# Input rows and modulation weights issued by ScalarE, modulation products in 32-column pieces

## The chip, the cores and the metric

The kernel runs on one core of one Trainium2 chip. The metric is the device time of one execution in microseconds (us), and of several runs the median. All arithmetic that matters here is fp32.

## The reference

The block is an adaLN layer around an S4D convolution and a token-mixing MLP, for L = 2048 tokens, D = 448 channels, N = 256 states, F = 1792 hidden units:

```python
mod = (_silu(c) @ w_mod).reshape(1, 6, 1, -1)        # c: 1 x 448, w_mod: 448 x 2688
sa, ca, ga, sb, cb, gb = mod[:, 0], ..., mod[:, 5]
h = _layernorm(x) * (1 + ca) + sa
x = x + ga * S4D(h)     # y = irfft(rfft(h) * rfft(K)) + h * D_skip, K = 2 Re sum_n C exp(A dt l)
h = _layernorm(x) * (1 + cb) + sb
x = x + gb * MLP(h)     # over the token axis: w2 gelu(w1 h + b1) + b2
```

The change concerns the six modulation vectors `mod[k]` (k = 0 to 5, each of 448 numbers, needed on all 128 partitions) and the way in which the input `x` and the matrix `w_mod` come into the chip's memory.

## The kernel before

The first part of the program makes the convolution kernel K in 56 half groups, one in each step `s` of a long loop, and lays the rest of the first part (layer norm, transforms, modulation) between them. Every eighth step begins with a `window(s)`, in which ScalarE (ACT) makes the eight magnitudes of the next steps (`mag`, L614). A step then has these pieces:

- PE: `st_kgen(s - 2)` (L678, 32 small products into 32-column tiles), then `st_phase(s + 1)` (L603), which fills two pairs of accumulators, `xe` and `xg`, for the next step. There are two of each, so the phase of step s + 1 needs those of step s - 1 to be free: `xg` is free when VectorE (DVE) has done its last product of that step (L657).
- ACT: six activations (L644 to L649) on `xe` and `xg`; the first is `ab`, the third writes what DVE reads first.
- GpSimd (POOL): two products `G` (L651, L652), and `w` and `m` of a later step (L630, L632).
- DVE: two products `E` (L653, L654), then whatever `between` gives it, then two more (L656, L657). For s = 2 to 7 `between` holds the statistics of rows 2s and 2s + 1 of the input (`u_stats`, L494), so these must have landed; and pieces of the next chain of exponents (L384 to L397).

In window 8 the input is normalised and from then on `u_rows` makes products `pu` of the input (L525), which DVE multiplies by a modulation (`yt`, L528). Such a product, the accumulators of the modulations (`pm`) and those of `y` share one pool of three.

PE, ACT, DVE and POOL run their instructions in the order in which the code is written. SyncE (SP), which issues most transfers, does so too until step 8; after that a scheduler orders it.

Transfers issued by SP or ACT take one of eight completion semaphores, `DMAHW0` to `DMAHW7`, in turn, one turn for both engines together. Where a transfer takes a semaphore that an earlier transfer has used, the issuing engine first waits until that earlier one has landed. Transfers issued by POOL have eight semaphores of their own.

The 16 rows that each partition holds of the input (`xt`) come in by `x_load(r0, n, eng)`, which issues four transfers of 32 partitions each. Rows 0 to 3 are issued by POOL early; rows 4 to 7 after step 0 and rows 8 to 15 after step 1, by POOL as well. The four blocks of `w_mod` for k = 0 to 3 come in by `wm_load`: k = 1 by SP before step 0, k = 2, 3 and 0 by POOL before steps 2, 3 and 5 (the table `late`). The blocks for k = 4 and 5 are loaded later into `xt` by SP.

`modulation(k)` is four accumulated products of 112 x 448 by `scb`, the silu of c copied along 128 columns, so that every partition gets the sum; ACT then copies the accumulator to `mod[k]`. k = 1, 2 and 3 are made in halves in steps 2 to 7, k = 0 in window 8, k = 4 and 5 at the head of window 16.

Of the kernel before, what the change touches and what calls it, by code (L numbers as in the profile page):

```python
# [11 lines left out]
F32 = mybir.dt.float32  # L12
# [9 lines left out]
L, D, N, F = 2048, 448, 256, 1792  # L22
P = 128
# [193 lines left out]
def tile_adaln_s4d_mixer(ctx, tc, i, out):  # L217
# [20 lines left out]
    with ExitStack() as es:  # L238
# [76 lines left out]
        def wm_load(k, tile, eng=nc.sync):  # L315
            wms[k] = tile
            eng.dma_start(wms[k], i["w_mod"][:, k * D : (k + 1) * D].rearrange("(q p) d -> p q d", p=PP))
# [11 lines left out]
        def wm_slot(k):  # L329
            w = wm0.rearrange("p k d -> p (k d)")[0:PP]  # L330
            return w[:, 4 * D * (k % 4) : 4 * D * (k % 4 + 1)].rearrange("p (q d) -> p q d", q=4)
# [1 line left out]


        late = {
            2: lambda: wm_load(2, wm_slot(2), G),
            3: lambda: wm_load(3, wm_slot(3), G),
            5: lambda: wm_load(0, wm_slot(0), G),
            6: lambda: [
                nc.sync.dma_start(wu, i["WU"]),  # L340
                nc.sync.dma_start(wc, i["WC"].rearrange("p (c m) -> p c m", c=2)),
# [127 lines left out]


        sc = qp.tile([PP, 4], F32, name="sc")
        scb = qp.tile([PP, 4, P], F32, name="scb")

        pmods = {}

        def modulation(k, *halves):
            if 0 in halves:
                pmods[k] = pms.tile([P, D], F32, tag="ms", name="pm")
            for h in halves:
                for q in (2 * h, 2 * h + 1):  # L480
                    T.matmul(pmods[k], scb[:, q], wms[k][:, q], start=q == 0, stop=q == 3)
            if 1 not in halves:
                return
            pm = pmods.pop(k)
            act.append(lambda: S.activation(mod[k], pm, AF.Copy, bias=1.0 if k in (1, 4) else 0.0))


# [320 lines left out]
        def remainder():  # L808

            ts(dt4[:, 1:4], dt[:, 1:4], 1.0 / (4 * math.pi), None, ALU.mult)  # L810
            ts(ldt2[:, 1:4], ldt[:, 1:4], 1.5 * math.log(2.0), None, ALU.add)

            ts(sc, sc, 1.0, None, ALU.add)
            V.reciprocal(sc, sc)
            tt(sc, sc, cvec, ALU.mult)
            V.tensor_copy(scb, sc[:, :, None].to_broadcast([PP, 4, P]))

# [97 lines left out]
        par_load(1)  # L917
        for g in (1, 2):
            load(g, False)
        wm_load(1, wm_slot(1))  # L920
        remainder()

        def chains():
# [46 lines left out]
        def window(s):  # L970
            angle()
            logs(s == 8)
            if s == 8:
                u_scale()
                u_norm(0)
                u_norm(1)

            if s in (8, 16):
                for k in (0,) if s == 8 else (4, 5):
                    modulation(k, 0, 1)  # L980
            if s == 0:
                st_exponents(s)
            for e in range(BATCH):
                st_exp(s + e)

                if e + 1 < BATCH:
                    st_exponents(s + e + 1)
                else:
                    st_phase(s)
                mellow()  # L990
                if s == 8 and e == 0:
                    tt(mod[1], mod[1], mod[2], ALU.mult)
                flush(dve)
                flush(act)
                if s < 32:
                    more(WPACE[s // 8][e])
                if s == 0 and e >= 4:
                    u_stats(e - 4)
                if s == 8 and e == 1:

                    tt(mod[0], mod[0], mod[2], ALU.mult)
                if s and e < (2 if s <= 32 else 1):
                    st_kgen(s - (2 if s <= 32 else 1) + e)
                elif e == 5:
                    if s == 8:
                        yks[0] = y0.tile([P, 32, DC], F32, tag="yk", name="yk0")
                    st_s1(s > 16)

                if s in (8, 16):
                    some(u_rows, rows, (2, 2, 2, 2, 2, 0, 1, 1)[e])  # L1010
                elif s == 24 and e != 5:
                    some(u_cols, cols, 1)

                if s >= 40 and e == 2:
                    piece(False)
                if s >= 32 and e in (4, 7):
                    piece(e == 4 and pieces[0] < NP, V)
                if s == 0 and e in (4, 5):
                    st_mag2(e - 4)
                elif s and (e < 2 or s >= 32):  # L1020
                    st_mag2(s + e)
                if s == 8 and e == 0:
                    u_norm(e + 2)
                if s == 0 and e == 3:
                    for r in range(4):
                        dsk_copy(r)
            if s == 0:

                S.activation(one, one, AF.Sin)
# [6 lines left out]
        for s in range(tail):  # L1036
# [23 lines left out]
            def between():  # L1060
# [4 lines left out]
                if s < len(pace):  # L1065
                    more(pace[s])

            mellow()
            if s >= NHALF:
                flush(dve)  # L1070
# [15 lines left out]


            if s < 2:
                x_load(4 + 4 * s, 4 + 4 * s, G)
            free = s > 7 and not st_s1(s % BATCH == BATCH - 1)  # L1090
            if s + 2 < 32 and (s + 2) % BATCH > 1:
                st_mag2(s + 2)

            if 1 < s < 8:
                modulation(s // 2, s % 2)
            if s == 7:
                par_load(2)

# [265 lines left out]
```

## Time and profile before

| | before |
|---|---|
| median of 3 runs | 715.01 us (712.2 to 716.16) |
| the profiled execution | 720.78 us, of it span 719.0 us |
| busy PE, DVE, ACT, POOL | 632.4, 453.2, 438.7, 273.6 us |
| mean granted TensorE clock | 0.921 |

The profile is of one execution. In a row of the timeline stand the start (us from the start of the span), the duration, the engine, the line of the code, the operation, what it writes and reads, and in brackets how long the engine had been idle and what ended that. Rows of SP and POOL with DMA are the issue of a transfer, not the transfer itself. PEclk in a table by windows is the granted TensorE clock, 1.00 for full speed.

### The profile page before, as it was taken

To read this page: it belongs to the slowest core of one execution; us is meant where nothing else is said; L and a number is where in the kernel's file an instruction comes from. 1 tells how busy PE (TensorE), PEld (TensorE's weight loads), DVE (VectorE), ACT (ScalarE), POOL (GpSimd) and SP (SyncE) were. 2 spreads that over 40 slices of the span, in tenths; PEclk is the share of its full clock that TensorE was granted. 3 is DMA by queue.
4 is the path that set the end of the run, shared out by engine and by line. 5 is a ranking of instruction groups with operands and counts; after the bars stand their busy time and mean duration, and the time that the engine had idled before them with its cause. 6 is when DMAs were issued, how large, how long until landed. Compare 5 with 4: busy or idle time off the path is not lost. (4 is left out here: it accounts for less than half of the span.)

```text
span 719.0 us, 18288 instructions
## 1 busy us (share of the span) xinstructions
PE 632.4 (88%) x7204; PEld 456.4 (63%) x7204; DVE 453.2 (63%) x875; ACT 438.7 (61%) x876; POOL 273.6 (38%) x328
## 2 busy tenths in 40 slices
PE   0659889979989888799888949999999999999997
PEld 0335335434535556566565617778999999999996
DVE  7469879679778668586684548778622263334441
ACT  5847588887987789989883549787522242222220
POOL 6486437528737787878785600000000000000000
PEclk9868857988998889999899959999999999999999
DMA  7795464266888635535236989974585436655540
GB/s 169 207 191 131 162 192 138 113 229 179 244 227 248 204 92 133 149 100 154 70 102 181 285 245 266 239 195 113 174 231 146 148 109 172 173 155 154 156 139 26
DMA packets 101635, 121.19 MB, mean 169 GB/s; under 512 B 13066, under 2 KB 87422, under 8 KB 101422
## 3 DMA queue, kind: packets, MB, share of 16 engines
q1 hardware_dynamic: 100014, 113.16, 55.2%
q0 software_dynamic: 1536, 6.87, 4.4%
q8 instruction: 57, 0.93, 0.6%
q14 instruction: 28, 0.23, 0.1%
HBM read 84.64 MB, written 34.87 MB: 166 GB/s over the span
## 5 line engine op out<-in xcount | busy, mean ns | idle before, releaser
L202 ACT CAST whi<-w 128x896 fp32r<-128x896 f32 x64 | 59.7, 938 | 131.4 <-PE o L1331 84.7
L651 POOL TENSOR_TENSOR G<-mag,gs 128x512 f32<-128x512 f32 x56 | 71.9, 1284 | 92.4 <-ACT gs L647 92.1
L211 DVE TENSOR_TENSOR wlo<-w,whi 128x896 fp32r<-128x896 f32 x64 | 68.0, 1087 | 40.3 <-ACT whi L202 31.0
L603 PE MATMUL xg<-tab,lph 64*128 64x512 f32 x112 | 68.8, 617 | 25.9 <-ACT xg L649 8.0
L1196 PE MATMUL acc<-h3h,whi 128*128 128x448 f32 x224 | 83.3, 372 | 0.1
L1197 PE MATMUL acc<-h3l,whi 128*128 128x448 f32 x224 | 81.9, 366 | 0.0
L1331 PE MATMUL o<-ul,whi 128*128 128x448 f32 x224 | 81.3, 363 | 0.0
L1330 PE MATMUL o<-uh,whi 128*128 128x448 f32 x224 | 81.2, 362 | 0.0
L1198 PE MATMUL acc<-h3h,wlo 128*128 128x448 f32 x224 | 80.9, 361 | 0.0
L1332 PE MATMUL o<-uh,wlo 128*128 128x448 f32 x224 | 80.6, 360 | 0.0
L678 PEld LDWEIGHTS kg<-E,G 128*32 128x32 f32 x3584 | 59.8, 119 | 32.3 <-issue 16.4
L603 PE MATMUL xe<-tab,lph 64*128 64x512 f32 x112 | 67.8, 609 | 12.2 <-ACT gs L648 10.2
L678 PE MATMUL kg<-E,G 128*32 128x64 f32 x3584 | 69.8, 235 | 2.2 <-issue 1.5
L652 POOL TENSOR_TENSOR G<-mag,gs 128x512 f32<-128x512 f32 x56 | 71.7, 1280 | 0.0
L653 DVE TENSOR_TENSOR E<-m,xe 128x512 f32<-128x512 f32 x56 | 38.3, 683 | 40.8 <-ACT xe L646 31.8
L632 POOL TENSOR_TENSOR m<-mag,w 128x512 f32<-128x512 f32 x56 | 59.9, 1070 | 6.0 <-DVE E L657 1.5
L1334 DVE SCALAR_TENSOR_TENSOR y<-o,b,mod 128x448 f32<-128x448 f32 x16 | 10.9, 684 | 80.3 <-PE o L1332 80.3
L644 ACT ACTIVATE ab<-xe 128x512 f32<-128x512 f32 x56 | 33.7, 601 | 30.3 <-PE xe L603 16.1
L1196 PEld LDWEIGHTS acc<-h3h,whi 128*128 128x128 f32 x224 | 42.3, 189 | 13.8 <-ACT h L1252 6.3
L603 PE MATMUL xe<-tab,lex 64*128 64x512 f32 x56 | 31.7, 575 | 18.8 <-POOL dsk L468 17.2
L614 ACT ACTIVATE mag<-xe 128x512 f32<-128x512 f32 x56 | 35.5, 634 | 19.7 <-PE xg L603 14.0
L603 PEld LDWEIGHTS xg<-tab,lph 64*128 64x128 f32 x112 | 24.3, 217 | 36.3 <-issue 10.3
(229 smaller groups left out, 1486.1 us busy)
## 6 DMA issues: line engine op xcount, KB each, us to landing
w<-in_B_w_dram SPq DMA_DIRECT2D x64, 224.0 KB
w<-in_B_w_dram SPq DMA_DIRECT2D x32, 448.0 KB
yu_d<-yt SPq DMA_DIRECT2D x16, 448.0 KB
yi<-yu_d SPq DMA_DIRECT2D x32, 224.0 KB
us_d<-uo SPq DMA_DIRECT2D x16, 448.0 KB
u<-us_d SPq DMA_DIRECT2D x32, 224.0 KB
v_d<-vt SPq DMA_DIRECT2D x32, 224.0 KB
vt<-v_d SPq DMA_DIRECT2D x16, 448.0 KB
```

What stands on the lines that cost most here:

```text
L211: eng.tensor_tensor(lo, w, hi.bitcast(F32), ALU.subtract)
L603: T.matmul(out[k], lhs[r], rhs[r], start=start, stop=stop)
L632: G.tensor_tensor(m2, me, w[:, :, None].to_broadcast([P, GD, 32]), ALU.mult)
L651: G.tensor_tensor(Gt[:, 1], mg_, v32(sg), ALU.mult)
L652: G.tensor_tensor(Gt[:, 0], mg_, v32(cg_), ALU.mult)
L678: T.matmul(kgs[g][32 * q : 32 * q + 32, m], Gt[:, c, d], E[:, c, d], start=h == 0 and c == 0 and m == 0, stop=h == 1 and c == 1, skip_grou ...
L1196: nc.tensor.matmul(acc[f], hi[:, fs], h3h[:, r], start=r == 0, stop=False)
L1197: nc.tensor.matmul(acc[f], hi[:, fs], h3l[:, r], start=False, stop=False)
L1198: nc.tensor.matmul(acc[f], lo[:, fs], h3h[:, r], start=False, stop=r == 15)
L1330: nc.tensor.matmul(o, hi[:, ks], uh[kh][:, k], start=kh == 0 and k == 0, stop=False)
L1331: nc.tensor.matmul(o, hi[:, ks], ul[kh][:, k], start=False, stop=False)
L1332: nc.tensor.matmul(o, lo[:, ks], uh[kh][:, k], start=False, stop=kh == 1 and k == 6)
```

## The change

The rows 4 to 15 come in three parts of four, all issued by ACT: the first part before the activations of step 0, the second after step 0, the third after step 1. The modulation weights for k = 0 to 3 are issued by ACT too: k = 1 and 2 after the third part, k = 0 before step 3, k = 3 before step 4. `modulation` becomes two functions. `mod_parts(k)` makes the four products side by side, each with 32 columns of `scb` and into 32 partitions of one accumulator, and ACT copies that accumulator to `mod[k]`. `mod_sum(k)` multiplies the copy by a matrix `add4` that has ones in rows 0, 32, 64 and 96 and so adds the four pieces on every partition; ACT writes `mod[k]` anew from that. DVE writes `add4` at the start of the program.

```diff
         late = {
-            2: lambda: wm_load(2, wm_slot(2), G),
-            3: lambda: wm_load(3, wm_slot(3), G),
-            5: lambda: wm_load(0, wm_slot(0), G),
+            2: lambda: wm_load(2, wm_slot(2), S),
+            3: lambda: wm_load(0, wm_slot(0), S),
+            4: lambda: wm_load(3, wm_slot(3), S),
...
-        scb = qp.tile([PP, 4, P], F32, name="scb")
-
-        pmods = {}
-
-        def modulation(k, *halves):
-            if 0 in halves:
-                pmods[k] = pms.tile([P, D], F32, tag="ms", name="pm")
-            for h in halves:
-                for q in (2 * h, 2 * h + 1):
-                    T.matmul(pmods[k], scb[:, q], wms[k][:, q], start=q == 0, stop=q == 3)
-            if 1 not in halves:
-                return
-            pm = pmods.pop(k)
+        scb = qp.tile([PP, 4, 32], F32, name="scb")
+        add4 = qp.tile([P, P], F32, name="add4")
+        V.memset(add4, 0.0)
+        for q in range(4):
+            V.memset(add4[32 * q : 32 * q + 1], 1.0)
+
+        def mod_parts(k):
+            pm = pms.tile([P, D], F32, tag="ms", name="pm")
+            for q in range(4):
+                T.matmul(pm[32 * q : 32 * q + 32], scb[:, q], wms[k][:, q], start=True, stop=True)
+            act.append(lambda: S.copy(mod[k], pm))
+
+        def mod_sum(k):
+            pm = pms.tile([P, D], F32, tag="ms", name="pm")
+            T.matmul(pm, add4, mod[k], start=True, stop=True)
             act.append(lambda: S.activation(mod[k], pm, AF.Copy, bias=1.0 if k in (1, 4) else 0.0))
...
-            V.tensor_copy(scb, sc[:, :, None].to_broadcast([PP, 4, P]))
+            V.tensor_copy(scb, sc[:, :, None].to_broadcast([PP, 4, 32]))
...
-        wm_load(1, wm_slot(1))
         remainder()
...
-            if s in (8, 16):
-                for k in (0,) if s == 8 else (4, 5):
-                    modulation(k, 0, 1)
+            if s == 16:
+                mod_parts(4)
+                mod_parts(5)
...
                     tt(mod[0], mod[0], mod[2], ALU.mult)
+                    mod_parts(3)
+                elif s == 8 and e == 2:
+                    mod_sum(3)
+                elif s == 16 and e == 0:
+                    mod_sum(4)
+                    mod_sum(5)
...
+            if s == 0:
+                x_load(4, 4, S)
             mellow()
...
             if s < 2:
-                x_load(4 + 4 * s, 4 + 4 * s, G)
+                x_load(8 + 4 * s, 4, S)
+            if s == 1:
+                wm_load(1, wm_slot(1), S)
...
-            if 1 < s < 8:
-                modulation(s // 2, s % 2)
+            if 4 < s < 8:
+                mod_sum((1, 2, 0)[s - 5])
+            if 4 <= s < 7:
+                mod_parts((1, 2, 0)[s - 4])
```

What this does to the order of an engine is seen at three places. On ACT at the start of step 0 (`one` ends window 0, `ab` begins the step; what an instruction waits for stands in brackets) there stood before:

```order
33 L1029 ACT_TABLE_LOAD
34 L1029 ACTIVATE one<-one 128x1
35 L644 ACTIVATE ab<-xe 128x512 [waits PE_49]
36 L645 ACTIVATE gs<-xg 128x512 [waits PE_49]
37 L646 ACTIVATE xe<-xe 128x512 [waits Activation_49]
```

And now:

```order
33 L1037 ACT_TABLE_LOAD
34 L1037 ACTIVATE one<-one 128x1
35 L292 DMA xt<-in_A_u_dram 32x1792 [waits DMAHW3_49]
36 L292 DMA xt<-in_A_u_dram 32x1792 [waits DMAHW7_49]
37 L292 DMA xt<-in_A_u_dram 32x1792 [waits DMAHW5_49]
38 L292 DMA xt<-in_A_u_dram 32x1792 [waits DMAHW3_49]
39 L647 ACTIVATE ab<-xe 128x512 [waits PE_49]
```

Four issues stand ahead of the step, the first and the fourth on the same semaphore. After step 1 six more stand ahead of `ab` of step 2 (of after, with the last two of the four of `xt` and both of `wm`):

```order
59 L292 DMA xt<-in_A_u_dram 32x1792 [waits DMAHW4_49]
60 L292 DMA xt<-in_A_u_dram 32x1792 [waits DMAHW3_49]
61 L317 DMA wm_79<-in_w_mod_dram 112x4x448 [waits DMAHW6_49]
62 L317 DMA wm_79<-in_w_mod_dram 112x4x448 [waits DMAHW7_49]
63 L647 ACTIVATE ab<-xe 128x512 [waits PE_49,Activation_49]
```

Their semaphores were last used by transfers of SP. On SP, from the loads of the second group's parameters on to the reloads for later steps (`lph` feeds the phases of two steps each, `lex` those of window 8), before:

```order
42 L271 DMA A_A_imag<-in_A_A_imag_dram 128x256 [waits DMAHW1_49]
43 L589 DMA lph_143<-pars_57 32x256 [waits DMAHW3_49,DMAHW2_49]
44 L593 DMA lph_143<-pars_57 64x1x256 [waits DMAHW5_49,DMAHW4_49]
45 L589 DMA lph_144<-pars_57 32x256
46 L593 DMA lph_144<-pars_57 64x1x256
47 L317 DMA wm_79<-in_w_mod_dram 112x4x448 [waits DMAHW6_49]
48 L589 DMA lph_142<-pars_57 32x256 [waits DMAHW7_49,PE_49]
```

And after, with the reloads that follow:

```order
42 L271 DMA A_A_imag<-in_A_A_imag_dram 128x256 [waits DMAHW3_49]
43 L592 DMA lph_143<-pars_57 32x256 [waits DMAHW4_49]
44 L596 DMA lph_143<-pars_57 64x1x256 [waits DMAHW6_49,DMAHW5_49]
45 L592 DMA lph_144<-pars_57 32x256 [waits DMAHW7_49]
46 L596 DMA lph_144<-pars_57 64x1x256 [waits DMAHW0_49]
47 L592 DMA lph_142<-pars_57 32x256 [waits DMAHW1_49,PE_49]
48 L596 DMA lph_142<-pars_57 64x1x256 [waits DMAHW2_49,PE_49]
49 L592 DMA lph_143<-pars_57 32x256 [waits DMAHW4_49,DMAHW2_49,PE_49]
50 L596 DMA lph_143<-pars_57 64x1x256 [waits DMAHW6_49,DMAHW3_49,PE_49]
51 L592 DMA lex_145<-pars_57 32x256 [waits DMAHW5_49]
52 L596 DMA lex_145<-pars_57 64x1x256 [waits DMAHW6_49]
53 L592 DMA lex_146<-pars_57 32x256 [waits DMAHW7_49]
```

The load of `wm` is gone from SP, and the semaphores have shifted: `A_A_imag` (row 42) now takes `DMAHW3` after ACT's first transfer of `xt`, and ACT's fourth takes it after `A_A_imag`. By the same count ACT's twelfth transfer of `xt` (`DMAHW3`, row 60) follows SP's row 50, which waits for the phase of step 3, and the two of `wm` follow SP's rows 52 and 53.

On PE at the head of window 16 (`y` ends the step before, `xe` and `xg` belong to the window, `kg` is st_kgen, `pu` feeds DVE) there stood before:

```order
356 L481 MATMUL pm<-xt,scb 128x448 x8
357 L603 MATMUL xe<-tab,lex_145 128x512
358 L603 MATMUL xg<-tab,lex_145 128x512
359 L678 MATMUL kg<-E,G 32x64 x32
360 L525 MATMUL pu<-xt,wu 64x448 x4
```

And now:

```order
358 L482 MATMUL pm<-xt,scb 32x448 x8
359 L606 MATMUL xe<-tab,lex_145 128x512
360 L606 MATMUL xg<-tab,lex_145 128x512
361 L487 MATMUL pm<-mod_69,add_175 128x448
362 L487 MATMUL pm<-mod_70,add_175 128x448
363 L681 MATMUL kg<-E,G 32x64 x32
364 L528 MATMUL pu<-xt,wu 64x448 x4
```

Eight products of 128 columns become eight of 32 columns, and two summing products come after the window's first phase, behind ACT's copies of the pieces. In steps 4 to 8 the same replacement is made one modulation at a time: parts in steps 4, 5, 6 (k = 1, 2, 0), sums in steps 5, 6, 7, and k = 3 in window 8.

## The prediction

> **What bounds the kernel now.** First the page's busy times, then the windows (us, busy of each engine with instructions, PEclk, DMA share, GB/s) around the steps that the change touches.
>
> ```profile
> PE 632.4 (88%) x7204; PEld 456.4 (63%) x7204; DVE 453.2 (63%) x875; ACT 438.7 (61%) x876; POOL 273.6 (38%) x328
> 40.00:51.00 11.00, 3.58 (x72) 1.80 (x69) 5.40 (x9) 3.48 (x7) 9.81 (x13) 0.77 1.00 209
> 51.00:60.00 9.00, 8.55 (x83) 4.47 (x83) 8.86 (x19) 3.63 (x7) 5.48 (x6) 0.52 0.75 136
> 60.00:71.00 11.00, 10.96 (x226) 6.02 (x222) 9.41 (x20) 9.83 (x20) 7.00 (x7) 1.00 0.49 132
> ```
>
> PE's 88% is an average. From 40 to 51 us PE, DVE and ACT all stand half idle or worse while the transfers are at 1.00; then PE is full, first at half clock. The queues' share of the transfers' time between 40 and 46 us says whose they are, and the timelines of POOL, DVE and PE what they hold up.
>
> ```profile
> q0 software_dynamic: 142, 1.32, 98.0%
> 32.64 2.01 POOL L292 DMA_DIRECT2D xt<-in_A_u_dram  x4
> 45.85 0.63 DVE L494 BATCH_NORM_STATS2 st<-xt 128x6 f32<-128x448 f32 x1 [5.53 <-DMA xt<-in_A_u_dram]
> 47.34 2.58 DVE L392 TENSOR_TENSOR ya<-ya,xa 128x256 f32<-128x256 f32 x1
> 50.67 0.67 DVE L657 TENSOR_TENSOR E<-m,xg 128x512 f32<-128x512 f32 x1
> 51.45 0.76 PE L603 MATMUL xg<-tab,lph 64*128 64x512 f32 x1 [7.87 <-issue]
> 53.45 3.35 PE L481 MATMUL pm<-wm,scb 112*128 112x448 f32 x4
> ```
>
> POOL issues rows 4 to 7 at 32.64 us, and they land 11 to 13 us later. DVE waits 5.53 us for them in step 2; with a slow product (2.58 us) behind that, step 2's last product ends at 51.34 us, and only then does `xg` come free for PE's phase of step 4. That stall would go with rows that land earlier. PE then pays 3.35 us for two modulation products at half clock.
>
> **The transfers.** The changed kernel takes them from POOL; ACT issues sixteen. The nearest prices are SP's: 0.59 us for the same 224 KB of `xt` later in the program, and for a block of `wm` the 0.43 us of an ordinary load (the third row).
>
> ```profile
> L1138 SPq DMA_DIRECT2D xt<-in_A_u_dram x16: 528/590/613, 409.1 to 471.0; - x16
> 1.20 0.42 SPq L271 DMA_DIRECT2D A_C_real<-in_A_C_real_dram  x1
> 1.66 0.43 SPq L271 DMA_DIRECT2D A_C_imag<-in_A_C_imag_dram  x1
> 3.31 0.42 ACT L851 ACTIVATE xa<-A_C_real 128x256 f32<-128x256 f32 x1 [1.29 <-DMA A_C_real<-in_A_C_real_dram]
> 5.04 0.42 ACT L852 ACTIVATE ya<-A_C_imag 128x256 f32<-128x256 f32 x1 [1.31 <-DMA A_C_imag<-in_A_C_imag_dram]
> SPq L593 <- DMA lex<-pars: 1.9, 1, 1.9
> ```
>
> Issue alone is 12 x 0.59 + 4 x 0.43 = 8.8 us of ACT. But the order shows a dearer thing: the shared completion semaphores make an issuing engine wait for another's transfer. The last row is such a wait in the kernel before: SP's load of `lph` stood 1.9 us until a load of `lex`, with which it has no data in common, had landed. Now ACT is in that turn, with its activations behind it. How long a landing takes on this queue: from 1.20 to 3.31 is 2.1 us for 128 KB, from 1.66 to 5.04 is 3.4 us beside others. I take 2.6 for the first two waits, where 224 KB parts run beside them, and 2.1 for the small load later; both ends stay for the range.
>
> ```profile
> 28.05 0.58 ACT L644 ACTIVATE ab<-xe 128x512 f32<-128x512 f32 x1
> 31.65 0.60 ACT L644 ACTIVATE ab<-xe 128x512 f32<-128x512 f32 x1
> 26.69 0.43 SPq L271 DMA_DIRECT2D A_A_imag<-in_A_A_imag_dram  x1
> 38.45 0.68 DVE L657 TENSOR_TENSOR E<-m,xg 128x512 f32<-128x512 f32 x1
> 40.63 0.49 SPq L593 DMA_DIRECT2D lph<-pars  x1
> 42.18 0.54 SPq L589 DMA_DIRECT2D lex<-pars  x1
> ```
>
> *Step 0.* ACT issues its first part at 28.05. SP, which came to `A_A_imag` at 26.69, must wait until that has landed: 30.65. `A_A_imag` lands 2.6 later, at 33.25, and only then goes ACT's fourth: `ab` begins at 33.84 instead of 28.05. Without the two waits it would be 28.05 + 4 x 0.59 = 30.41.
>
> *Step 1.* A step and what stands behind it took 3.60 us (28.05 to 31.65); four issues add 2.36. `ab` of step 1: 39.80 (31.65 before). Its sixth activation ends 3.1 later, two products of DVE take 1.3: its last product ends at 44.2. PE's phase of step 3 follows, and SP's reload of `lph` behind that phase started 1.5 us after that product (39.13 to 40.63): here at 45.7.
>
> *Step 2.* ACT is free at 42.9 and has issued three parts by 44.7. The twelfth waits for that reload; the two of `wm` wait for the `lex` loads behind it. SP issued the last of these 1.55 us after the reload (40.63 to 42.18), so here at 45.7 + 1.55 = 47.25; it lands 2.1 later, and with one issue of 0.43 `ab` of step 2 stands at 49.8. DVE now needs three activations (1.5), two products (1.2), then what took 5.49 from 45.85 to 51.34. The statistics find their rows landed, at no cost, and the slow product (2.58 us beside POOL's work) I price at 1.2 like L384 in the row below: 5.49 - 2.58 + 1.2 = 4.1. Step 2 ends at 56.6 against 51.34: 5.3 later.
>
> ```profile
> 31.79 1.18 DVE L384 TENSOR_TENSOR s<-xa,ya 128x256 f32<-128x256 f32 x1 [0.80 <-ACT ya L383]
> 54.85 0.68 DVE L657 TENSOR_TENSOR E<-m,xg 128x512 f32<-128x512 f32 x1
> 65.26 0.68 DVE L657 TENSOR_TENSOR E<-m,xg 128x512 f32<-128x512 f32 x1
> 69.71 0.68 DVE L657 TENSOR_TENSOR E<-m,xg 128x512 f32<-128x512 f32 x1
> 73.56 0.68 DVE L657 TENSOR_TENSOR E<-m,xg 128x512 f32<-128x512 f32 x1
> ```
>
> *Steps 3 to 7.* From step 2's to step 7's last product went 22.9 us (50.67 to 73.56), of which steps 4 and 5 held DVE behind PE's products at half clock. With those products gone or halved DVE sets the pace: 4.18 (50.67 to 54.85), then 4.45 and 3.85 by turns (the last three rows), in all 4.18 + 4.45 + 3.85 + 4.45 + 3.85 = 20.8. So 2.1 come back, and step 7 ends 3.2 us late. The two `wm` issues in steps 3 and 4 lie beside DVE's work; without that cover they cost 0.9.
>
> **The products.** Two whole products took 1.77 us at full clock (60.28 below), one is 0.88. For four side by side the nearest row is `pu` of the same 448 columns in small tiles: 0.98 us; its other end is no overlap, 3.5 us.
>
> ```profile
> 60.28 1.77 PE L481 MATMUL pm<-wm,scb 112*128 112x448 f32 x4
> 71.12 4.78 PE L481 MATMUL pm<-wm,scb 112*128 112x448 f32 x12
> 77.29 1.32 PE L525 MATMUL pu<-xt,wu 32*64 32x448 f32 x8
> 79.99 0.98 PE L525 MATMUL pu<-xt,wu 32*64 32x448 f32 x8
> 78.53 1.16 DVE L528 TENSOR_TENSOR yt<-pu,mod 128x448 f32<-128x448 f32 x2 [2.28 <-PE pu L525]
> 136.92 6.28 PE L481 MATMUL pm<-xt,scb 112*128 112x448 f32 x16
> 143.56 1.10 PE L678 MATMUL kg<-E,G 128*32 128x64 f32 x64
> 139.03 0.58 ACT L614 ACTIVATE mag<-xg 128x512 f32<-128x512 f32 x1
> 140.24 0.54 ACT L485 ACTIVATE mod<-pm 128x448 f32<-128x448 f32 x1 [0.62 <-PE pm L481]
> 145.60 1.16 DVE L528 TENSOR_TENSOR yt<-pu,mod 128x448 f32<-128x448 f32 x2 [6.83 <-PE pu L525]
> ```
>
> In steps 5 and 6 a sum and the parts of the next (0.88 + 0.98) replace 1.77: nothing. ACT's extra copies (0.54) end before the sums are due while DVE sets the pace; a sum without that cover waits about 1 us. *Window 8:* six products, 71.12 to 75.90, held the first `pu`, for which DVE waited 2.28. Only the sum for k = 0 stays there. Now step 7's last product (74.24) is late next: behind it come phase, st_kgen and `pu`, as from 75.90 to 78.61, so 76.9 instead of 78.53: 1.6 won. The parts and the sum of k = 3 lie where PE waits for DVE. *Window 16:* DVE waits 6.83 for PE. The parts end at 136.92 + 1.96 = 138.9. ACT has its magnitudes done at 139.6, its copies at 140.1 and 140.7, and the sums end at 140.94 + 0.88 = 141.8, where `kg` begins, against 143.56: 1.8 won. DVE's four writes of ones and the clearing lie before 3.31 us, where it waits for `A_C_real` as ACT does, and I cost them at nothing, 0.8 without that cover.
>
> **The sum.** 3.2 - 1.6 - 1.8 = -0.2 us. From the profiled execution, 720.78 us (span 719.0 and 1.78 around it), that is 720.6; the same difference from the median of the three runs, 715.01, gives 714.8. The profiled execution is 0.8% above that median, so I carry the difference, not the level. About 0.5%, 3.6 us, is what a measurement of this kernel can tell from no change.
>
> **The rivals.** *The semaphore waits do not bind* (the turn is the program's, but landings may be so short that ACT arrives later than they do). Then `ab` of step 0, 1, 2 stands at 30.4, 36.4 and 42.7, 7.1 us earlier than in the sum, and DVE follows: 707.7. For it: at the 381 GB/s of the row below 224 KB pass in 0.6 us. Against it: even the small load of 1.20 needed 2.1 us to its landing, and here two follow each other.
>
> *Transfers are as slow from ACT as from POOL.* ACT's first part decides: if it lands not in 2.6 us but in the 8.1 that POOL's needed in the median, `A_A_imag`, and behind it every step, is 5.5 us later: 720.3. It is slower than before from a landing of 6.4 us on.
>
> ```profile
> xt<-in_A_u_dram POOLq DMA_DIRECT2D x8, 224.0 KB, 8.1
> 24.00:25.00 1.00, 1.00 (x4) 0.59 (x3) 0.00 (x0) 1.00 (x4) 0.00 (x0) 1.00 1.00 381
> ```
>
> Against it stands the last row: with SP's transfers alone 381 GB/s flowed, against 209 in the stretch in which POOL's ruled. The Trainium skill, DMA: Bandwidth & Descriptors, section "Issuing engines are not separate DMA queues", speaks for it: whoever issues, the same 16 engines move the data, and another issuer saves only sequencer time. The two rates above differ, so here the issuer's queue seems to matter; no row shows ACT's own.
>
> *Half clock stays.* From the products of step 4 (60.28) to those of step 7 (71.12) PE was busy throughout, 3.6 us a step. If PE, with gaps of several us in steps 2 and 3, is still at half clock in steps 5 and 6, the ratio of 3.35 to 1.77 makes that 6.8, against DVE's 4.2: 2.6 more in each, 5.2 in all, 720.0. It decides if PEclk is under about 0.9 there. For it: 0.52 from 51 to 60. Against it: 1.00 from 60 on, after about 7 us of work. The Trainium skill, TensorE: Matmul & The Clock Gate, Part 1, would give full clock after some 3.4 us of steady work; the trace shows twice that.
>
> **How the numbers follow.** Forecast 0.40, waits that don't bind 0.25, slow transfers 0.20, half clock 0.15. Within the forecast the landings at 2.1 or 3.4, the slow product between 0.5 and 2.6 and the parts between 0.98 and 3.5 move it by some 3 us either way: 0.06 of it falls below 711.4, 0.05 above 718.6. So faster 0.06 + 0.25 = 0.31, same 0.29, slower 0.05 + 0.20 + 0.15 = 0.40. The range of 707 to 722 leaves out a tenth at each end: earlier issues with still shorter landings, and two of the slower cases together. The forecast's own range is 711 to 718.
>
> **What would show it.** Right: ACT idle ahead of its fourth and twelfth transfer and of `wm`, put down to a DMA; DVE's statistics in step 2 without a wait; DVE's last product of step 7 near 77 us; window 16's first `kg` 4.9 us after `y`, not 6.6. Wrong: `ab` of step 2 before 44 us, or ACT's 224 KB parts landing after 7 us or more, or parts that take over 2 us a set.

## The result, and the profile after

| | before | after |
|---|---|---|
| median | 715.59 us of 4 runs (712.2 to 718.02) | 723.63 us of 4 runs (721.33 to 724.89) |
| ratio, with its 95% interval | 1 | 1.0101 (1.0065 to 1.0136) |
| the profiled execution | 720.78 us, span 719.0 | 723.94 us, span 722.1 |

The change costs 1.0%, some 7 us; forecast was no change within 0.5%. The code lines of a step's pieces stand 3 higher than before (`ab` is L647, DVE's last product of a step L660, `pu` L528, `yt` L531); the products of the modulations are at L482 and L487.

The page's busy times after the change:

```profile
PE 623.5 (86%) x7216; PEld 452.3 (63%) x7216; DVE 451.6 (63%) x880; ACT 441.5 (61%) x882; POOL 266.7 (37%) x317
```

PE has 8.9 us less to do, and the program takes longer: the loss lies elsewhere. The windows over the same stretches as before:

```profile
40.00:51.00 11.00, 6.38 (x143) 4.26 (x143) 5.66 (x7) 1.03 (x3) 3.93 (x5) 0.99 0.49 109
51.00:60.00 9.00, 0.76 (x1) 0.28 (x1) 4.39 (x10) 6.11 (x13) 3.90 (x5) 0.50 0.84 195
```

Between 40 and 51 us the transfers are at half load now (1.00 before), and ACT, the fourth of the busy columns, works 1.03 us out of 11. PE then has a single product from 51 to 60. ACT's timeline shows why (ACTq is its queue of issues):

```profile
25.88 0.39 ACTq L292 DMA_DIRECT2D xt<-in_A_u_dram  x1
33.43 0.38 ACTq L292 DMA_DIRECT2D xt<-in_A_u_dram  x1
33.86 0.60 ACT L647 ACTIVATE ab<-xe 128x512 f32<-128x512 f32 x1 [5.39 <-DMA A_A_imag<-in_A_A_imag_dram]
37.94 0.60 ACT L647 ACTIVATE ab<-xe 128x512 f32<-128x512 f32 x1 [0.35 <-ACT ya L383]
40.75 10.90 ACTq L292 DMA_DIRECT2D xt<-in_A_u_dram  x3
52.88 0.88 ACTq L317 DMA_DIRECT2D wm<-in_w_mod_dram  x2
53.86 0.60 ACT L647 ACTIVATE ab<-xe 128x512 f32<-128x512 f32 x1 [12.84 <-DMA xt<-in_A_u_dram]
```

There are two holds. Ahead of step 0 ACT stands 5.4 us, until `A_A_imag` has landed and its fourth issue may go; ahead of step 2 it stands 12.8 us. The bracket names the last transfer, not the cause: the third part of `xt` is held inside the 10.90 us of its group, then the weights from 51.65 to 52.88. Who is waited for stands on SP's queue:

```profile
29.93 0.33 SPq L271 DMA_DIRECT2D A_A_imag<-in_A_A_imag_dram  x1
46.80 0.31 SPq L592 DMA_DIRECT2D lph<-pars  x1
47.21 0.49 SPq L596 DMA_DIRECT2D lph<-pars  x1
48.34 0.49 SPq L596 DMA_DIRECT2D lex<-pars  x1
```

By the order, ACT's twelfth transfer takes the semaphore of the `lph` load of 47.21, and the two blocks of weights those of the `lex` loads of 48.34 and 48.87. The trace's records of landings show the counts of each semaphore. The `lph` load landed at 51.31, 4.1 us after its issue, and ACT's twelfth issue, the last of its group of three, began at 51.33. The `lex` loads landed at 52.86 and 53.17, after 4.5 and 4.3 us, and the blocks went at 52.88 and 53.26. DVE, which the held step feeds, and the first `yt` of window 8:

```profile
41.56 1.21 DVE L388 TENSOR_SCALAR s<-s 128x256 f32<-128x256 f32 x1
42.81 1.75 DVE L390 RECIPROCAL xa<-s 128x256 f32<-128x256 f32 x1
45.02 0.68 DVE L660 TENSOR_TENSOR E<-m,xg 128x512 f32<-128x512 f32 x1
55.54 0.69 DVE L656 TENSOR_TENSOR E<-m,xe 128x512 f32<-128x512 f32 x1 [9.84 <-ACT xe L649]
56.74 0.62 DVE L497 BATCH_NORM_STATS2 st<-xt 128x6 f32<-128x448 f32 x1
58.23 0.57 DVE L392 TENSOR_TENSOR ya<-ya,xa 128x256 f32<-128x256 f32 x1
59.57 0.67 DVE L660 TENSOR_TENSOR E<-m,xg 128x512 f32<-128x512 f32 x1
81.09 0.68 DVE L660 TENSOR_TENSOR E<-m,xg 128x512 f32<-128x512 f32 x1
86.67 1.16 DVE L531 TENSOR_TENSOR yt<-pu,mod 128x448 f32<-128x448 f32 x2 [3.05 <-PE pu L528]
```

The old stall is gone: the statistics (56.74) wait for nothing, and the product behind them takes 0.57 us instead of 2.58. But step 2 begins 17.3 us later than before and its last product ends at 60.24 against 51.34, step 7's at 81.77 against 74.24, and `yt` begins at 86.67 against 78.53. The lag is carried on: `ab` of step 16 stands at 162.50 against 155.38.

### The profile page after: what moved, and what is told of

Read it like the earlier page. It is cut to its first block, busy times and chain, and to the rows that moved or that the text cites. A ratio compares the mean times of both kernels' runs of the same rounds, so it can differ in the third digit from the quotient of the medians.

```text
span 722.1 us, 18309 instructions
## 1 busy us (share of the span) xinstructions
PE 623.5 (86%) x7216; PEld 452.3 (63%) x7216; DVE 451.6 (63%) x880; ACT 441.5 (61%) x882; POOL 266.7 (37%) x317
## 5 line engine op out<-in xcount | busy, mean ns | idle before, releaser
L681 PEld LDWEIGHTS kg<-E,G 128*32 128x32 f32 x3584 | 61.6, 122 | 31.8 <-issue 20.7
L656 DVE TENSOR_TENSOR E<-m,xe 128x512 f32<-128x512 f32 x56 | 38.3, 684 | 53.9 <-ACT xe L649 47.7
L647 ACT ACTIVATE ab<-xe 128x512 f32<-128x512 f32 x56 | 33.6, 601 | 38.2 <-DMA xt<-in_A_u_dram 12.8
L606 PEld LDWEIGHTS xe<-tab,lph 64*128 64x128 f32 x112 | 24.0, 215 | 43.8 <-ACT gs L651 20.3
```

The lines of the kernel that those rows point to most:

```text
L606: T.matmul(out[k], lhs[r], rhs[r], start=start, stop=stop)
L681: T.matmul(kgs[g][32 * q : 32 * q + 32, m], Gt[:, c, d], E[:, c, d], start=h == 0 and c == 0 and m == 0, stop=h == 1 and c == 1, skip_grou ...
```

## The experiments

All ratios are against the kernel before on the same chip. The four columns behind them are from each profiled execution: `ab` of step 2, the end of DVE's last product of step 7, the first `yt`, `ab` of step 16.

| kernel | ratio (95% interval) | ab 2 | step 7 ends | first yt | ab 16 |
|---|---|---|---|---|---|
| before, first profile / e8 | 1 | 36.54 / 36.18 | 74.24 / 73.51 | 78.53 / 77.79 | 155.38 / 153.31 |
| after | 1.0101 (1.0065 to 1.0136) | 53.86 | 81.77 | 86.67 | 162.50 |
| e1 products only | 0.9998 (0.9960 to 1.0036) | 36.19 | 72.67 | 77.57 | 157.76 |
| e5 SP issues, old products | 1.0017 (0.9990 to 1.0045) | 35.94 | 73.59 | 77.85 | 155.04 |
| e2 SP issues, new products | 0.9943 (0.9899 to 0.9987) | 36.25 | 68.18 | 74.22 | 147.15 |
| e7 the same, weights first | 0.9966 (0.9931 to 1.0000) | 35.63 | 67.28 | 72.93 | 146.22 |
| e3 only x from ACT | 1.0048 (1.0011 to 1.0085) | 50.91 | 78.39 | 83.56 | 156.82 |
| e4 all but the first part from ACT | 1.0081 (1.0039 to 1.0124) | 52.67 | 80.57 | 85.49 | 158.53 |
| e6 third part after step 2 | 1.0107 (1.0071 to 1.0144) | 42.22 | 81.20 | 87.25 | 161.13 |
| e9 e7 with other edits | 0.9959 (0.9918 to 1.0000) | 36.47 | 69.90 | 75.82 | 151.93 |
| e10 only the first part from ACT, first time | 0.9893 (0.9831 to 0.9956) | - | - | - | - |
| e11 only the weights from ACT | 1.0069 (1.0035 to 1.0103) | 36.76 | 78.73 | 85.18 | 157.96 |
| e12 = e2 again | 0.9926 (0.9896 to 0.9956) | 36.89 | 69.50 | 75.46 | 148.25 |
| e13 only the first part from ACT | 0.9919 (0.9887 to 0.9951) | 40.86 | 68.77 | 74.80 | 150.58 |
| e14 = after again | 1.0108 (1.0068 to 1.0149) | 54.01 | 81.25 | 86.64 | 161.52 |

**The two halves of the change, each alone.** The theory: ACT's holds make the loss. e1 keeps the new products and gives the transfers back to POOL (and `wm` for k = 1 to SP):

```diff
-            2: lambda: wm_load(2, wm_slot(2), S),
-            3: lambda: wm_load(0, wm_slot(0), S),
-            4: lambda: wm_load(3, wm_slot(3), S),
+            2: lambda: wm_load(2, wm_slot(2), G),
+            3: lambda: wm_load(0, wm_slot(0), G),
+            5: lambda: wm_load(3, wm_slot(3), G),
...
-            if s == 0:
-                x_load(4, 4, S)
...
-                x_load(8 + 4 * s, 4, S)
+                x_load(4 + 4 * s, 4 + 4 * s, G)
```

> The modulations in pieces with sums, as in the change; the transfers issued as before (POOL and SP), only that POOL loads the weights for k = 0 before those for k = 3, since k = 0 is now made first. The theory that the whole loss comes from ACT being held ahead of steps 0 and 2: this kernel has no holds, so it must not be slower than before; 1 to 3 us faster (the sum had 1.6 + 1.8 for windows 8 and 16, the trace of after shows 1.1 for window 16). The rival that the products in pieces cost time (window 8 of after ran at half clock and gave nothing): 0 to 3 us slower than before.

0.9998: no difference, where 1 to 3 us were expected to be won. There is no hold, and no loss; but no gain either. The rows still come late from POOL, as the waits of DVE show (what waits, for what, us, times, longest):

```profile
DVE st L497 <- DMA xt<-in_A_u_dram: 5.2, 1, 5.2
```

That is not all: its first `yt` comes no later than in the kernel before, but `ab` of step 16 then follows 3.3 to 4.7 us later behind it. Its granted clock from 71 to 160 us was 0.73, in the two profiles of the kernel before 0.80 and 0.82. Whether the products in pieces bring that about was not tested apart.

e2 keeps the new products and has SP issue all sixteen transfers at the same places of the program:

```diff
-            2: lambda: wm_load(2, wm_slot(2), S),
+            2: lambda: wm_load(2, wm_slot(2), nc.sync),
...
-                x_load(4, 4, S)
+                x_load(4, 4, nc.sync)
...
-                x_load(8 + 4 * s, 4, S)
+                x_load(8 + 4 * s, 4, nc.sync)
...
-                wm_load(1, wm_slot(1), S)
+                wm_load(1, wm_slot(1), nc.sync)
```

> The changed kernel with the same sixteen transfers at the same places of the program, issued by SP instead of ACT. The theory of the holds: ACT waits for no transfer, ab of steps 0, 1, 2 begins at about 28, 31.7 and 36 us, the rows have landed when DVE needs them, and the time is 6 to 10 us below before (705 to 709), 14 to 18 below after. The rival that the transfers themselves are the loss (big parts in the way of SP's small loads): the phase of step 2 or 4 then waits for lph, and the time stays at that of after or between.

0.9943: faster than before by some 4 us (6 to 10 were expected), and 1.6% under the changed kernel. ACT's waits in this stretch name no DMA any more. The issuer alone turns a loss of 1% into a gain. e5 has SP issue them with the old `modulation` (and, as before, the weights for k = 1 ahead of step 0 and those for k = 3 ahead of k = 0):

```diff
-        def mod_parts(k):
...
-        def mod_sum(k):
...
+        def modulation(k, *halves):
```

> All sixteen transfers issued by SP as in the kernel with all on SP, but the modulations as before (four accumulated products of 128 columns, in the steps where they stood), with the weights for k = 1 loaded where they stood and those for k = 3 ahead of k = 0. The theory that the products in pieces are worth 1 to 2 us in window 16 and nothing in window 8, where POOL's normalisation of the first rows is late next: 1 to 2 us slower than the kernel with all on SP, 712 to 714. The rival that the pieces are worth nothing or cost the clock: 708 to 711.5. Either way below before, since ACT is not held.

The gain that was looked for here did not come: 1.0017. The old products are made two steps earlier than the new ones, and now they wait for weights that are queued behind the rows, with DVE behind them. From the waits of PE and DVE in e5:

```profile
PE pm L481 <- DMA wm<-in_w_mod_dram: 3.7, 1, 3.7
DVE E L653 <- PE pm L481: 5.2, 1, 5.2
```

So neither half wins alone; together, without ACT, they win 0.6 to 0.7%.

**Where the hold goes.** If single transfers that ACT issues made the wait, taking those away would shorten it. e3 leaves ACT only the rows:

```diff
-            2: lambda: wm_load(2, wm_slot(2), S),
+            2: lambda: wm_load(2, wm_slot(2)),
...
-                wm_load(1, wm_slot(1), S)
+                wm_load(1, wm_slot(1))
```

> The changed kernel with the four blocks of weights issued by SP; the twelve transfers of x stay on ACT. By the count of the semaphores ACT's fourth then waits only for a load that SP issues before any wait for ACT, and its twelfth for ACT's own seventh, no longer for SP's reload of lph. The theory of the holds: the 12.8 us ahead of step 2 go, and the first hold shrinks from 5.4 to about 2; step 7 ends 7 to 12 us earlier than in after, the time is at or below before (706 to 714). The rival that issuing on ACT costs it time as such: twelve of sixteen issues are still there, so at most a quarter of the loss of 8 goes, 721 or more.

A miss: the holds were expected to go, and there are three now. ACT's waits:

```profile
ACT ab L647 <- DMA wm<-in_w_mod_dram: 6.3, 1, 6.3
ACT ab L647 <- DMA A_log_A_real<-in_A_log_A_real_dram: 4.8, 1, 4.8
ACT ab L647 <- DMA xt<-in_A_u_dram: 4.6, 1, 4.6
```

They make 15.7 us in all, against 18.2 in the changed kernel, and the loss is half as large (1.0048). The longest of the three is a wait of ACT, with its rows alone, for a long transfer of weights that SP has issued, which took its turn between ACT's own. e4 takes only the first part from ACT:

```diff
-                x_load(4, 4, S)
+                x_load(4, 4, nc.sync)
```

> The changed kernel with the first part of x (rows 4 to 7) issued by SP, the rest by ACT. SP's A_A_imag then waits for no transfer of ACT, but the twelfth and the two of weights still wait for SP's reloads behind the phase of step 3. The theory of the holds: the 5.4 us ahead of step 0 go, the hold ahead of step 2 stays at 10 to 13, because the phase of step 3 comes earlier by as much as steps 0 and 1 do; the time is 4 to 6 us below after (718 to 720). The rival that only the second hold counts, the first being slack: no change from after, 722 to 725.

A miss again. The hold ahead of step 0 is gone (one of 1.1 us stands ahead of step 1), but the one ahead of step 2 grows from 12.8 us by most of that:

```profile
ACT ab L647 <- DMA xt<-in_A_u_dram: 16.3, 1, 16.3
```

In this kernel SP issued the `lph` load, on which by the order the last transfer of the third part waits, at 42.39, 4.8 us earlier than in the changed kernel; ACT's group of four still ended only at 50.43 (40.24 + 10.19). The records of landings show that this load did end the wait: it landed at 50.10, after 7.7 us instead of 4.1, and ACT's last issue of `xt` began at 50.12. e6 puts the third part and the first two weights behind step 2's activations:

```diff
-                x_load(8 + 4 * s, 4, S)
-            if s == 1:
+                if s == 0:
+                    x_load(8, 4, S)
+            if s == 2:
+                x_load(12, 4, S)
                 wm_load(1, wm_slot(1), S)
+                wm_load(2, wm_slot(2), S)
```

> The changed kernel, all sixteen transfers by ACT, but the third part of x and the weights for k = 1 and 2 come after step 2 instead of after step 1, those for k = 0 and 3 before step 4. The theory of the holds: the waits for SP's reloads then stand ahead of step 3 and not of step 2, so that DVE has a step's work of 4 us more while ACT is held; step 7 ends 3 to 5 us earlier than in after, 718 to 721. The rival that the number of transfers on ACT or their traffic is what costs: nothing changes, 723 or more.

A miss as well: 1.0107, the time that the rival had. The hold ahead of step 0 stays, and the other only moves behind, ahead of step 3, with 10.3 us. The weights were issued later too, PE waited 1.8 us for them, and step 7 ended where it did in the changed kernel. e11 is the opposite of e3, ACT issues the weights and SP the rows:

```diff
-                x_load(4, 4, S)
+                x_load(4, 4, nc.sync)
...
-                x_load(8 + 4 * s, 4, S)
+                x_load(8 + 4 * s, 4, nc.sync)
```

> The kernel with all of x on SP and the four blocks of weights issued by ACT as in the change. By the count of the semaphores ACT's four then wait only for transfers that have landed long before. The theory of the holds, and that an issue on ACT that does not wait is free: ab of step 2 not held, step 7 at 67 to 69, time within 1.5 us of the kernel with all on SP (710 to 713). The rival that an issue on ACT costs by itself, or that the weights' traffic does: 714 or more.

Also a miss: ACT is nearly free of waits for transfers (1.7 us) and still this costs 0.7%, the time that the rival had. Now SP is the one that waits; the waits of SP, PE and ACT, and DVE's timeline:

```profile
SPq L292 <- DMA wm<-in_w_mod_dram: 15.2, 3, 9.7
...
PE xe L606 <- DMA lph<-pars: 9.9, 1, 9.9
...
ACT ab L647 <- PE xe L606: 18.6, 5, 12.2
...
59.40 0.63 DVE L497 BATCH_NORM_STATS2 st<-xt 128x6 f32<-128x448 f32 x1 [8.58 <-DMA xt<-in_A_u_dram]
```

SP's issues of `xt` stand up to 9.7 us behind ACT's `wm`, so DVE's statistics of step 4 wait 8.6 us for their rows; the `lph` loads are queued behind them on SP, PE's phase of step 6 waits 9.9 us for those, and ACT 12.2 us for PE. Both in e3 and in e11, with one turn for two queues, one of them waits for the other's long transfers; what counts is what is queued behind the one that waits. That an issue on ACT costs something by itself is not excluded by e11, but nothing in its trace points to it.

**Does the first hold cost anything?** The prediction handed every us of it down. e10 is e2 with the first part issued by ACT:

```diff
-                x_load(4, 4, nc.sync)
+                x_load(4, 4, S)
```

> The kernel with all transfers on SP, but the first part of x (rows 4 to 7, four transfers) issued by ACT ahead of step 0 as in the change. The theory of the holds: ACT is held once, about 5 us ahead of step 0, behind A_log_A_real or A_A_imag; every step is later by that, step 7 ends near 73.5 instead of 68.2, and the time is 4 to 6 us above the kernel with all on SP, about as before. The rival that the first hold is slack: step 7 within 1 us of that kernel, 711 to 713.

0.9893 (0.9831 to 0.9956), not slower than e2. e13 repeats it beside e12 (e2 once more) and e14 (the changed kernel), all three on one chip.

> The kernel of e2_all_on_SP once more, beside e13 and e14 on the same chip. Both theories: ratio 0.990 to 0.998 to the kernel before, step 7 ending near 68 us.

> The kernel of e10 once more. Theory A, the first hold is slack (the weights land too late for step 6 anyway): ratio within 0.003 of e12's, step 7 within 1.5 us of e12's. Rival B, the hold is handed down: 4 us or 0.006 above e12's ratio, step 7 near 72 us.

> The changed kernel once more. Theory A, the second hold (12.8 us ahead of step 2) makes the loss alone: ratio 1.007 to 1.013, so 0.012 to 0.020 above e12 and e13 alike. Rival B, both holds share in it: e13 stands halfway between e12 and e14.

e12 0.9926, e13 0.9919, e14 1.0108: the first hold is slack, as far as these intervals of 0.3% either way can tell. In e13 it is there, on ACT's timeline, and gone by step 6:

```profile
32.41 0.60 ACT L647 ACTIVATE ab<-xe 128x512 f32<-128x512 f32 x1 [4.87 <-DMA A_log_A_real<-in_A_log_A_real_dram]
54.74 0.60 ACT L647 ACTIVATE ab<-xe 128x512 f32<-128x512 f32 x1 [1.87 <-PE xe L606]
58.80 0.60 ACT L647 ACTIVATE ab<-xe 128x512 f32<-128x512 f32 x1 [0.24 <-PE xg L606]
```

In e12, without it, `ab` of step 5 stands 4.7 us earlier and that of step 6 0.7 us later, on ACT's timeline:

```profile
50.03 0.60 ACT L647 ACTIVATE ab<-xe 128x512 f32<-128x512 f32 x1 [0.79 <-PE xe L606]
59.54 0.60 ACT L647 ACTIVATE ab<-xe 128x512 f32<-128x512 f32 x1 [1.27 <-PE xg L606]
```

because PE has to wait for weights there, on its timeline:

```profile
54.41 1.72 PE L482 MATMUL pm<-wm,scb 112*32 112x448 f32 x8 [4.25 <-DMA wm<-in_w_mod_dram]
```

A start that is 4 us earlier only arrives earlier at that wait. (At `ab` of step 16 e13 stands 2.3 us behind e12, about what two profiles of one kernel differ by; see e8.) e14 has both holds, 5.1 us and this one:

```profile
ACT ab L647 <- DMA xt<-in_A_u_dram: 13.6, 1, 13.6
```

and its step 7 ends 12.5 us behind e13's. From e13 to e14 the later parts and the weights move to ACT, and with them comes the second hold; the two kernels lie 1.9% apart. The issues themselves took little of ACT's time (0.48 us for four, below), so the hold ahead of step 2 is what makes the loss. No run has all these issues on ACT without a hold.

**Can the gain be made larger?** e7 is e2 with the weights for k = 1 issued ahead of the third part:

```diff
-            if s < 2:
-                x_load(8 + 4 * s, 4, nc.sync)
+            if s == 0:
+                x_load(8, 4, nc.sync)
             if s == 1:
                 wm_load(1, wm_slot(1), nc.sync)
+                x_load(12, 4, nc.sync)
```

> The kernel with all transfers on SP, the weights for k = 1 ahead of rows 12 to 15. There PE waited 2.5 us in step 4 for those weights and DVE then 3.1 us; rows 12 to 15 are needed only in step 6. If this wait sets the pace: 2 to 3 us faster, 708.5 to 709.5. If SP's small loads behind it (lph, lex) are late next: no change, 711 to 712.

Step 7 ends earlier still (67.28), but its ratio, 0.9966, is not under e2's, and less came than was expected: the first `pu` now waits for its own weights `wu`, 2.8 us. e9 is e7 with `wu` and `wc` loaded in step 1 as well and row 1 normalised by DVE instead of POOL:

```diff
-                G.tensor_scalar(xt[:, r], xt[:, r], rs[:, r : r + 1], nm[:, r : r + 1], ALU.mult, ALU.add)
+                eng = V if r == 1 else G
+                eng.tensor_scalar(xt[:, r], xt[:, r], rs[:, r : r + 1], nm[:, r : r + 1], ALU.mult, ALU.add)
...
+                nc.sync.dma_start(wu, i["WU"])
+                nc.sync.dma_start(wc, i["WC"].rearrange("p (c m) -> p c m", c=2))
                 x_load(12, 4, nc.sync)
```

> The kernel with all transfers on SP and the weights for k = 1 first, with two more edits for the first pu of window 8: WU and WC are loaded in step 1 (there PE waited 2.8 us for WU), and the second row of each normalised row's pair number 1 goes to DVE instead of POOL (row 1 alone), since POOL's four rows of 0.78 us stood between DVE and the first pu. If these two set the start of window 8: the first yt stands 1 to 2 us earlier behind step 7 than the 5.6 there, 709 to 710.5. If the half clock that follows a gap on PE takes it back: no change.

0.9959, nothing more than e7: the wait for `wu` is gone, but PE waits 2.3 us for POOL's row at the first `pu` and 3.2 us for `lph` in two places, and step 7 ends 2.6 us later; from there to the first `yt` it is 5.9 us, in e7 5.7. The kernels of e12 and e13 are the fastest found, and cannot be told apart. e8 is the kernel before, for a second profile:

> The kernel before, unchanged, for a second profile. The first one took 720.78 us, well above the median of 715 to 716. The theory that the two differ only behind step 16, by the granted clock: steps 0 to 16 stand within 0.5 us of the first profile, the rest differs by several us.

It took 714.6 us in a single run, span 712.8. Up to step 7 it stands within 1.2 us of the first profile (0.7 at the end of that step), and at step 16 2.1 ahead of it, where 0.5 was expected; the rest of the 6.2 us between the two spans came later. So the difference of the first two spans, 722.1 - 719.0 = 3.1, understates the loss; against e8 it is 9.3, and what the ratio gives, some 7 us, lies between.

## Why the prediction was wrong

**Right.** The mechanism: ACT is idle ahead of its fourth and its twelfth transfer and ahead of `wm`, put down to a DMA. DVE's statistics of step 2 find their rows. `ab` of step 0 stands at 33.86 (33.84 predicted). A set of parts takes 0.96 us (0.98). In window 16 the parts, the sums and the first `kg` on PE's timeline:

```profile
145.13 0.96 PE L482 MATMUL pm<-xt,scb 112*32 112x448 f32 x8
148.29 1.77 PE L487 MATMUL pm<-mod,add 128*128 128x448 f32 x4 [0.46 <-ACT mod L483]
150.00 1.10 PE L681 MATMUL kg<-E,G 128*32 128x64 f32 x64
```

`kg` starts 4.87 us after the start of the parts (4.9 predicted, 6.64 before). Of those 1.8 us 1.1 are left at `ab` of step 16.

**Step 0, right by chance in part.** ACT issued its first part at 25.88, not at 28.05: issues run ahead of the activations. That 2.2 us was used up by longer landings, 4.0 us for the part (25.88 to 29.93) and 3.5 for `A_A_imag` (29.93 to 33.43), where 2.6 each was taken. And as e13 shows, the hold itself is slack once the rest is not held.

**Step 1, the issues.** Four issues were costed at 2.36 us of ACT. Between `ab` of step 0 and step 1 lie 4.08 us instead of 3.60: they cost 0.48. So `ab` of step 1 came 1.9 us earlier than predicted (37.94 against 39.80). But DVE's last product then ended 7.8 us after that `ab`, not 4.4: the step "its sixth activation ends 3.1 later, two products of DVE take 1.3" left out the chain of exponents on DVE in between (L388 and L390, 1.21 and 1.75 us, and their forerunners). The rows quoted of before had it, 7.5 us from 31.65 to 39.13. SP's reload followed that product by 1.5 us as said, at 47.21 instead of 45.7.

**Step 2, the term that failed.** "It lands 2.1 later": the small loads, priced by one that had landed alone at the start of the program, took 4.1 to 4.5 us. `ab` of step 2 came at 53.86, predicted 49.8. The prediction's last load, at 42.18 before, is the one of 48.87 (47.25 predicted). So the 4.1 us are 1.6 of a later load, 2.2 of its landing (4.3 against 2.1) and 0.3 from there to `ab`. The later load is the chain of exponents in step 1, 3.4 us, less the 1.9 that the cheap issues gave back. At the end of step 2 3.6 of them were left (60.24 against 56.6). The upper end of the range, 3.4 us from a row that stood in the same fence, was still too low.

Traffic of big parts beside the loads was not, in the main, what made them late. By the trace's records of packets none over 1 KB was in flight from 48.3 to 52.2 us, and the window shows the transfers at a quarter of their load (0.23, the last number but one):

```profile
48.30:52.20 3.90, 0.00 (x0) 0.00 (x0) 0.00 (x0) 0.00 (x0) 0.00 (x0) 0.83 0.23 64
```

The loads came in packets of 1 KB, and in more than half of this time at most two were in flight at once. The one that gave the 2.1 us had another shape, 128 rows of 1 KB. A nearer price stood in the trace of the kernel before: there the `lph` loads of 64 KB issued at 27.69 and 28.79, of the shape of those of 47.21 and 48.34, landed 4.5 and 5.8 us later.

**Steps 3 to 7** took 21.5 us against 20.8, so step 7 ended 7.5 us late, not 3.2.

**Window 8, the other term that failed.** "Step 7's last product is late next" promised 1.6 us; from that product to the first `yt` there were 4.3 us before and are 4.9 now. The normalisation of the rows on POOL in the kernel before, and after:

```profile
75.75 3.13 POOL L512 TENSOR_SCALAR xt<-xt,rs,nm 128x448 f32<-128x448 f32 x4 [2.95 <-DVE nm L503]
```

```profile
83.11 3.10 POOL L515 TENSOR_SCALAR xt<-xt,rs,nm 128x448 f32<-128x448 f32 x4 [3.81 <-DVE nm L506]
```

And PE after the change:

```profile
81.82 0.79 PE L606 MATMUL xg<-tab,lex 64*128 64x512 f32 x1 [1.73 <-DVE E L660]
82.55 1.93 PE L681 MATMUL kg<-E,G 128*32 128x64 f32 x64
84.41 2.24 PE L528 MATMUL pu<-xt,wu 32*64 32x448 f32 x8
```

`pu` needs a normalised row, and POOL begins on the first 1.5 us after step 7's product before, 1.3 us after now. What cost the time instead is PE itself: no longer kept busy by six products, it waits 1.73 us for step 7 and then runs at half clock, 1.93 us for `kg` (1.10 in the row of window 16) and 2.24 for `pu` (1.32 before). The granted clock stands behind POOL's column in these windows, the first of before, the others of after:

```profile
72.00:79.00 7.00, 7.00 (x91) 3.52 (x92) 4.12 (x14) 5.76 (x13) 4.05 (x6) 1.00 0.26 75
```

```profile
78.20:81.60 3.40, 1.72 (x4) 0.48 (x3) 3.33 (x8) 3.38 (x8) 1.11 (x1) 1.00 0.01 2
81.60:85.00 3.40, 3.18 (x69) 2.38 (x73) 1.66 (x8) 3.10 (x8) 1.89 (x3) 0.50 0.00 0
```

In e12 the normalisation does bind: PE waits 1.9 us for POOL's row, and `yt` comes 6.0 us after step 7. That half clock follows a stretch in which PE worked half the time is what the rows show; it was not varied by itself.

**The rivals.** "The waits do not bind" put the change without them 7.3 us under the median; e12 and e13 reach 0.74% and 0.81%, 5.3 and 5.8 us. "Transfers are as slow from ACT as from POOL" put its weight on the first part, whose first transfer landed in 4.0 us and which is slack. But the sign of being wrong, parts that land after 7 us or more, did come: by the records of landings seven of ACT's twelve took 7.1 to 8.7 us, the others 4.0 to 6.4. It cost nothing that the trace shows, as the rows were there when DVE needed them; and SP's twelve in e12 took 7.9 to 10.1 us, POOL's four for rows 4 to 7 in the kernel before 8.8 to 11.5 (the prediction's 11 to 13 counts from each issue to the landing of the last). The half clock did stay, but in window 8, not in steps 5 and 6.

In sum: 3.6 us too little at step 2, 0.7 in the steps behind it, 2.2 in window 8 and 0.7 in window 16 are 7.2 us, against the 7.2 that the ratio of 1.0101 makes of 715.01 us. That the two agree so closely is in part luck, since two profiles of the kernel before differ by 2.1 us at step 16 and by 6.2 in all.

## What to carry to other kernels

Before an engine that computes is given transfers to issue, follow the turn of the completion semaphores: a transfer that meets a load issued late by another queue holds all that is queued behind it, and giving some of the transfers back to that queue only changes who waits for whom. Give the issues to a queue with nothing but transfers behind it, and price a landing by the same load, in the same shape, elsewhere in the trace, not by another that landed alone. Where a wait is taken away, look for the next one on the same path before its gain or loss is handed down: 4.9 us ahead of step 0 cost nothing that the ratios show; with the hold of 13.6 us ahead of step 2 a gain of 0.8% became a loss of 1.1%.

## What was not expected of the hardware

Issues without a wait cost ACT almost nothing: they take 0.32 to 0.46 us on its queue while earlier activations still run, and four of them lengthened a step by 0.48 us. A landing is as late as its last part. In the trace's records most transfers count their semaphore up sixteen times. In the changed kernel the part of `xt` issued at 40.06 has fourteen counts from 43.02 to 43.82 us and the last two at 46.70 and 47.24, the one issued at 40.75 fourteen from 44.01 to 44.79 and the last two at 47.32 and 47.96. From 45.4 to 47.7 us there were hardly ever more than three packets in flight. So the mean load of the transfer engines, 0.49 in the window from 40 to 51 us, said nothing of a landing. The 64 KB loads of `lph` and `lex` show three counts only, for the `lph` load of 47.21 one at 48.12 and two at 51.30 and 51.31. It looks as if their data came in two streams and the tails of the other transfers stood in the same two; the trace does not name the engine of a packet, so this is left open.
